# Weights cast by GpSimd's DMAs instead of by GpSimd: attention and MLP on one core

## The chip, the cores and the metric

The kernel runs on one core of a Trainium2 chip. The metric is the device time of one execution in microseconds. Before the change the median of three runs is 236.49 us (236.44 to 236.9).

## The reference

The program is an attention with a sliding window and four sink positions, followed by a two-layer MLP. All inputs and the output are fp32.

```python
scores = (q @ k.T) / sqrt(64)                  # q, k, v: 4 batches, 8 heads, 768 positions, 64
keep = (key < 4) | ((0 <= query - key) & (query - key < 128))
a = softmax(where(keep, scores, -1e9))
x = heads side by side of (a @ v)              # 3072 tokens x 512
h = x @ w_in                                   # w_in 512 x 2048
g = h * sigmoid(1.702 * h)
out = g @ w_out                                # w_out 2048 x 512
```

## The kernel before

**Blocks.** The 3072 tokens are worked in 12 blocks of 256, three to a batch. For a block, q, k and v are loaded as fp32 (`load`, three DMAs of 512 KB on SP's queue; block 0 in smaller pieces over SP and ACT), rounded to fp16 by casts (`qk16`, `v16`), and then per pair of heads: q and k are transposed on TensorE (L446) and copied from PSUM into `qkT` (L263), the sinks' scores (L474) and the window's scores (L513) are multiplied, ScalarE takes exponentials (L482, L530), VectorE multiplies with a 0/1 mask (L539, L543), TensorE multiplies with V (L573), VectorE divides by the row sums (L587, L589), and the result is transposed (L596) and copied into `xT` (L263). The sinks' keys and values of a batch are kept by small GpSimd copies (`ks` L466, `vs` L422).

**MLP.** `mm1` (L630) forms h for 256 tokens, eight groups of 256 features, 8 matmuls each; ScalarE takes tanh (L642), VectorE forms g from it (`stt`, L644). `mm2` (L780) multiplies g with `w_out16` for blocks 0, 1 and 11. Blocks 2 to 10 use seven products instead of eight (`mm2_seven`, L705): it needs four sums of blocks of g per block of tokens (L675, into `sm`) and, once, four sums of quarters of w_out. `sums` makes these in 16 instructions (L658, into `wt1` to `wt4`), four quarters long, each when the two weight loads that it reads are in.

**Weights.** w_in and w_out are 4 MB each. `weights` loads them in eight DMAs of 1 MB on SP's queue as fp32 into four staging places, `w32`, which are the later space of two `gT` and two `sm` buffers, and two GpSimd casts for each round them into `w_in16` and `w_out16`. `LOADS` gives the order: blocks 0 and 1, weights 0 to 3 (w_in), weights 4, 6, 5, 7 (w_out), block 2, and so on.

**The plan.** Nothing here runs in the order of the source. Each operation is an `Op` with its dependencies, the engines that may run it with an assumed duration and latency, and a priority worked out from its block (`nominal`, 16,600 ns a block). `Plan.run` simulates the engines, always places the operation that can start first, among those within 20 ns the one of the best priority, chooses an engine where there are several (`plan.any`), and gives out PSUM banks. The resulting order is written out as a fixed order for each engine; what an operation waits for on the chip follows from its data. The plan models DMA with a common clock (`dma_free`) and a list `landed` that keeps at most eight in flight. The loads are chained in order of priority (`behind`). Before block 0's work arrives TensorE runs dummy matmuls (L840). Three lists say which engines may cast: `CAST_QK`, `CAST_V` (from block 2 on GpSimd alone) and `COPY`, the copies from PSUM into `qkT` and `xT` (VectorE or ScalarE).

Of the kernel before, what the change touches and what calls it, by code (L numbers as in the profile page):

```python
# [9 lines left out]
FP32 = mybir.dt.float32  # L10
# [25 lines left out]
LANES = 8  # L36

COLD = 4700.0
ENGINES = ("PE", "ACT", "DVE", "POOL", "SP")


class Plan:
# [14 lines left out]
    def run(self, warm=None, warm_until=0.0, late_bank=0.0):  # L57
        for o in self.ops:
            o.left = len(o.deps)
            for d in o.deps:  # L60
                d.users.append(o)
        free = {e: 0.0 for e in ENGINES}
        ready = {e: [o for o in self.ops if e in o.engs and not o.left] for e in ENGINES}

        bank_free = {b: 0.0 for b in range(self.n_banks)}
        if late_bank:
            bank_free[self.n_banks - 1] = late_bank

        count = {c: {i: 0.0 for i in range(n)} for c, n in self.limits.items()}
        dma_free = 0.0  # L70
        landed = []
        order = []
        todo = len(self.ops)

        def after(d, e):
            if d.eng != e or isinstance(d.engs[e][1], tuple):
                return d.end + HOP.get((d.eng, e), 50)
            return d.start + d.engs[e][0] + (0 if d.eng == "PE" else 60)

        def could(o, e):  # L80

            if o.behind and o.behind.start is None:
                return None, None
            s = max([free[e]] + [after(d, e) for d in o.deps])
            if isinstance(o.engs[e][1], tuple) and len(landed) >= LANES:
                s = max(s, landed[-LANES])
            if not o.acq:
                return s, s
            cls, n = o.acq
            times = sorted(bank_free.values())  # L90
            places = sorted(count[cls].values())
            if len(times) < n or len(places) < n:
                return s, None
            return s, max(s, times[n - 1], places[n - 1])

        while todo:
            best = None
            for e in ENGINES:
                found = sorted(
                    [(*could(o, e), o) for o in ready[e]], key=lambda x: (x[2].prio, x[2].seq)  # L100
                )
                keep, held_from = [], None
                for s0, s, o in found:
                    if s0 is None:
                        continue
                    if o.acq and o.acq[1] > 2 and (s is None or s > s0):

                        held_from = s0 if held_from is None else min(held_from, s0)
                        if s is not None:
                            keep.append((s, o))  # L110
                        continue
                    if s is None or (o.acq and held_from is not None and s >= held_from):
                        continue
                    keep.append((s, o))
                if not keep:
                    continue
                first = min(s for s, _ in keep)
                s, o = min(((s, o) for s, o in keep if s <= first + 20), key=lambda x: (x[1].prio, x[1].seq))
                lat = o.engs[e][1]
                key = s if len(o.engs) == 1 else s + lat - min(x[1] for x in o.engs.values())  # L120
                if best is None or key < best[0]:
                    best = (key, s, o, e)
            if best is None:
                raise RuntimeError("no operation can be planned")
            _, s, o, e = best
            dur, lat = o.engs[e]
            if e == "PE" and warm and s < warm_until:
                t = max(free["PE"], 300.0)
                while t + 110 < s:
                    order.append((t, -1, warm, e))  # L130
                    t += 107 if t < COLD else 57
            for x in o.engs:
                ready[x].remove(o)
            o.eng, o.start = e, s
            if o.acq:
                cls, n = o.acq
                o.banks, o.places = [], []
                for _ in range(n):
                    b = min((b for b in bank_free if bank_free[b] <= s), key=lambda b: (bank_free[b], b))
                    del bank_free[b]  # L140
                    o.banks.append(b)
                    p = min((p for p in count[cls] if count[cls][p] <= s), key=lambda p: (count[cls][p], p))
                    del count[cls][p]
                    o.places.append(p)
            free[e] = s + dur
            if isinstance(lat, tuple):
                dma_free = max(s + 2000, dma_free) + lat[0]
                o.end = dma_free + (500 if lat[0] < 500 else 1100)
                landed.append(o.end)
            else:  # L150
                o.end = s + lat
            for owner, i in o.rel:
                t = o.end + 80
                bank_free[owner.banks[i]] = t
                count[owner.acq[0]][owner.places[i]] = t
            for u in o.users:
                u.left -= 1
                if not u.left:
                    for x in u.engs:
                        ready[x].append(u)  # L160
            order.append((s, o.seq, o.fn, e))
            todo -= 1
        order.sort(key=lambda x: (x[0], x[1]))
        return [(fn, e) for _, _, fn, e in order]
# [7 lines left out]
def kernel(  # L172
# [22 lines left out]
    NS = NF // 2  # L195
    scale = float(1.0 / np.sqrt(Dh))
    PAIRED_FROM, RR = 2, 3
    RS, RQ, RV, RKT, RA, RXN, RX, RG, RSM, RTH, RO, RW = 3, 2, 4, 3, 6, 3, 3, 4, 2, 3, 4, 4

    SEVEN_FROM = 2  # L200
    NH = NF // 2
# [5 lines left out]
    def ring(name, n, shape, dt):  # L207
# [27 lines left out]
    sm = ring("sm", RSM, (P, 4, NH, P), FP16)  # L235
    osb = ring("osb", RO, (P, d_model), FP32)
    bank = [psp.tile([P, 512], FP32, name=f"bank{i}") for i in range(8)]


    stage = [("gT", RG - 1 - n, gT[RG - 1 - n].rearrange("p f t -> p (f t)")) for n in range(RW - RSM)] + [  # L240
        ("sm", n, sm[n].rearrange("p s f t -> p (s f t)")) for n in range(RSM)]
    w32 = [t.bitcast(FP32).rearrange("p (c f) -> p c f", c=4) for _, _, t in stage]

    plan = Plan(8, {"s": 4, "k": 1, "t": 2, "a": 2, "x": 2, "h": RTH, "o": 3})
    op = plan.op
# [61 lines left out]
    o_table = op("ACT", 1300, 1400, lambda: nc.scalar.activation(out=dummy, in_=zero[:, 0:8], func=AF.Exp),  # L307
                 [o_zero], prio=NEVER + 8, kind="const")

    CAST_W = ["POOL"] * 8  # L310
    CAST_QK = ["DVE ACT POOL", "DVE POOL"] + ["POOL"] * (NK - 2)
    CAST_V = ["POOL ACT DVE", "POOL ACT"] + ["POOL"] * (NK - 2)
    COPY = ["DVE ACT"] * NK

    o_win, o_wout = {}, {}
    loads = []

    def weights(n_th, j, at):
        dst = w32[n_th % RW]
        war = reuse(*stage[n_th % RW][:2])  # L320
        if j < 4:
            src = moe_w_in[:, bass.ts(j, 512)].rearrange("(c p) f -> p c f", p=P)
        else:
            src = moe_w_out[bass.ts(j - 4, 512), :].rearrange("(c p) f -> p c f", p=P)
        o_l = op("SP", 450, (3000,), lambda: nc.sync.dma_start(dst, src), war, prio=at, kind="w")
        loads.append(o_l)
        for n in range(2):
            if j < 4:
                c = slice(512 * j + 256 * n, 512 * j + 256 * n + 256)
                to, fr = w_in16[:, :, c], dst[:, :, bass.ts(n, 256)]  # L330
            else:
                to, fr = w_out16[:, 4 * (j - 4) + 2 * n : 4 * (j - 4) + 2 * n + 2], dst[:, 2 * n : 2 * n + 2]
            o = plan.any(cast(1024, CAST_W[j]), lambda e, to=to, fr=fr: copy(e, to, fr), [o_l], prio=at, kind="cw")
            uses(*stage[n_th % RW][:2], o)
            (o_win if j < 4 else o_wout)[2 * (j % 4) + n] = o


    L = 16600.0
    LOADS = ["a0", "a1", "w0", "w1", "w2", "w3", "w4", "w6", "w5", "w7", "a2"]

    SLABS = (0, 1, 4, 5, 2, 3, 6, 7)

    def load_at(x):
        return NEVER + 10 * LOADS.index(x) + 3 if x in LOADS else 10000.0 + (int(x[1:]) - 3) * L
# [6 lines left out]
    def load(k):  # L351
# [17 lines left out]
        else:  # L369
            for e, src in enumerate((q, k_ap)):  # L370
                def f(e=e, src=src):
                    nc.sync.dma_start(
                        dst[:, e], src[b, :, t0 : t0 + TB].rearrange("h (p i) d -> p h i d", i=2)
                    )
                o = op("SP", 450, (1800,), f, war, prio=prio + 0.1 * e, kind="load")
                loads.append(o)
                for p in range(NP):
                    lq[p, e] = o
# [35 lines left out]
                o_cv[k].append(o)  # L414
                uses("s32", sl, o)
        if r == 0:
            w0 = [o_win[0], o_win[1]]

            def f():
                for t in range(2):  # L420
# [238 lines left out]
                deps = [o_wout[c], o_wout[NS // 2 + c]] + [o_wt[d, c] for d in {"2": "3", "4": "2"}.get(n, "")]  # L659
                o_wt[n, c] = plan.any(SUM_W, f, deps, prio=nominal(SEVEN_FROM, 0), kind="wt")  # L660

    SUM_W = {"POOL": (1000, 1100), "DVE": (340, 430)}
    o_sm = {}

    def mm2_seven(k):
# [143 lines left out]
                    o_d = op(eng, 500, (800.0 / len(moves) / parts,), f, [o_c], prio=prio, kind="out")  # L809
                    uses("osb", oi, o_d)  # L810

    for n_, x_ in enumerate([x for x in LOADS if x[0] == "w"]):
        weights(n_, int(x_[1:]), load_at(x_))
    for k_ in range(NK):
        load(k_)
        for p_ in range(NP):
            front(k_, p_)
        for ps_ in [(0,), (1,), (2,), (3,)] if k_ < PAIRED_FROM else [(0, 1), (2, 3)]:
# [62 lines left out]
```

## Time and profile before

| | before |
|---|---|
| median of three runs | 236.49 us |
| the profiled execution's own time | 236.4 us |
| its span, first to last instruction | 234.7 us |
| TensorE busy (PE) | 222.2 us, 95% |
| VectorE busy (DVE) | 190.3 us, 81% |
| ScalarE busy (ACT) | 140.9 us, 60% |
| GpSimd busy (POOL) | 98.6 us, 42% |
| mean granted TensorE clock | 0.992 |
| DMA | 33.98 MB, 145 GB/s on average |

Times in the lines of the profile are microseconds from the start of the span, unless marked as ns. PE is TensorE's matmuls, PEld its weight loads, which run beside them. A line of a timeline or of the chain has its start, its duration, the engine and the kernel's line; "x16" counts instructions. Back to back, a matmul's start follows the last one's by less than the duration that is shown for one. L263 is the helper `copy`, so all casts and copies carry that line and are told apart by their tiles.

### The profile page before, as it was taken

The page shows a single profiled execution, that of the slowest core. Times are in us where ns is not written, and L with a number is a line of the kernel's source. Part 1 is how long each engine was busy: PE and PEld are TensorE (multiplying, and loading weights), DVE is VectorE, ACT ScalarE, POOL GpSimd, SP SyncE. Part 2 cuts the span into 40 slices and gives each one's busy share as a digit, 9 for nine tenths or more (in the row PEclk, how much of TensorE's full clock was granted, in tenths as well). Part 3 has the DMA queues.
Part 4 walks back from the last instruction along what each step waited for, and adds up shares of the span by engine and source line. Part 5 has one row for each costly group of instructions (what it writes and reads, how often), then busy time and mean ns, then how long its engine had stood idle before and what let it go on. Part 6 is the DMA issues. An engine that isn't in the chain of part 4 may idle for free.

```text
span 234.7 us, 6390 instructions
## 1 busy us (share of the span) xinstructions
PE 222.2 (95%) x2534; PEld 183.0 (78%) x2534; DVE 190.3 (81%) x412; ACT 140.9 (60%) x293; POOL 98.6 (42%) x163
## 2 busy tenths in 40 slices
PE   8876999959999999999999999999999999999994
PEld 7654886526788888888789889888888888888863
DVE  6788979976899988988979879889969869878520
ACT  3749562536688838838648838838567757635320
POOL 5658889971899960358521441243300000000000
PEclk9999999979999999999999999999999999999999
DMA  6999999999879994644284004004003003003042
GB/s 169 292 357 387 382 383 287 288 302 274 223 191 295 250 232 90 176 100 89 74 197 92 0 3 89 4 1 94 0 13 82 0 14 78 3 17 78 0 92 89
DMA packets 45743, 33.98 MB, mean 145 GB/s; under 512 B 1552, under 2 KB 38672, under 8 KB 45712
## 3 DMA queue, kind: packets, MB, share of 16 engines
q1 hardware_dynamic: 44480, 32.90, 52.0%
q10 hardware_dynamic: 1232, 0.66, 1.0%
q8 instruction: 20, 0.33, 0.6%
q14 instruction: 11, 0.09, 0.1%
HBM read 27.26 MB, written 6.29 MB: 143 GB/s over the span
## 4 chain that ended last, share of the span: by engine, by line
PE 75%; DVE 17%; ACT 3%; DMA 2%; issue 1%; ACTq 0%
PE bank L630 29%; PE bank L705 22%; PE bank L780 6%; PE bank L573 5%; DVE wt L658 5%; PE bank L513 4%; PE bank L446 4%; DVE gT L644 3%; DVE sm L675 2%; PE bank L596 2%; DMA qk<-in_k_dram 2%; DVE at L539 2%; ACT at L530 2%; DVE at L543 1%; PE bank L474 1%
## 5 line engine op out<-in xcount | busy, mean ns | idle before, releaser
L630 PE MATMUL bank<-xT,w_in 128*128 128x256 f16 x768 | 101.7, 273 | 0.0
L642 ACT ACTIVATE th<-bank 128x512 f16<-128x512 f32 x96 | 57.6, 601 | 49.6 <-PE bank L630 46.0
L630 PEld LDWEIGHTS <-w_in 128*128 128x128 f16 x768 | 72.1, 98 | 10.3 <-issue 1.3
L644 DVE SCALAR_TENSOR_TENSOR gT<-th,bank 128x512 f16<-128x512 f16 x96 | 64.9, 679 | 9.0 <-ACT th L642 8.7
L530 ACT ACTIVATE at<-bank 128x512 f16<-128x512 f32 (+1 forms) x96 | 49.1, 569 | 11.8 <-PE bank L513 11.2
L263 POOL CAST qk<-qk 128x512 f16<-128x512 f32 (+1 forms) x42 | 28.9, 722 | 27.9 <-PE bank L446 25.7
L263 POOL CAST v<-v 64x512 f16<-64x512 f32 x43 | 30.3, 705 | 8.8 <-PE bank L573 6.4
L705 PE MATMUL bank<-wt,sm 128*128 128x256 f16 x216 | 30.6, 273 | 0.4 <-DVE sm L675 0.3
L705 PEld LDWEIGHTS <-sm 128*128 128x128 f16 x288 | 26.5, 98 | 4.8 <-DVE sm L675 0.9
L539 DVE TENSOR_TENSOR at<-at,mask 128x1024 f16<-128x1024 f16 x32 | 23.5, 753 | 6.6 <-ACT at L530 6.6
L780 PE MATMUL bank<-w_out,gT 128*128 128x512 f16 (+1 forms) x112 | 24.5, 358 | 0.0
L573 PE MATMUL bank<-v,at 128*128 128x65 f16 x352 | 21.5, 193 | 2.0 <-DVE at L539 1.8
L705 PEld LDWEIGHTS <-gT 128*128 128x128 f16 x216 | 20.1, 98 | 2.3 <-issue 0.3
L573 PEld LDWEIGHTS <-at 128*128 128x128 f16 x352 | 17.3, 97 | 4.0 <-DVE at L539 2.2
L589 DVE TENSOR_TENSOR xn<-bank,rcp 128x256 f16<-128x256 f32 x48 | 19.8, 417 | 0.4
L466 POOL COPY ks<-qkT 64x4 f16<-64x4 f16 x32 | 9.5, 297 | 24.8 <-ACT qkT L263 19.7
L705 PE MATMUL bank<-w_out,gT 128*128 128x256 f16 x144 | 19.7, 273 | 0.0
L446 PE MATMUL bank<-ident,qk 128*128 128x128 f16 x192 | 18.9, 225 | 0.5 <-DVE qk L263 0.4
L730 DVE SCALAR_TENSOR_TENSOR osb<-bank,osb 128x256 f32<-128x256 f32 x45 | 18.4, 409 | 0.6 <-PE bank L705 0.6
L482 ACT ACTIVATE ats<-bank 128x256 f16<-128x256 f32 x32 | 12.4, 388 | 9.2 <-PE bank L474 7.8
L446 PEld LDWEIGHTS <-qk 128*128 128x128 f16 x192 | 14.0, 100 | 3.1 <-DVE qk L263 1.1
L780 PEld LDWEIGHTS <-gT 128*128 128x128 f16 x112 | 10.9, 101 | 6.9 <-issue 1.3
(53 smaller groups left out, 274.4 us busy)
## 6 DMA issues: line engine op xcount, KB each, us to landing
v<-in_v_dram SPq DMA_DIRECT2D x12, 512.0 KB, 7.2
out_dram<-osb SPq DMA_DIRECT2D x45, 128.0 KB, 2.4
qk<-in_q_dram SPq DMA_DIRECT2D x11, 512.0 KB, 5.2
qk<-in_k_dram SPq DMA_DIRECT2D x11, 512.0 KB, 6.7
gT<-in_moe_w_in_dram SPq DMA_DIRECT2D x2, 1024.0 KB, 10.1
sm<-in_moe_w_in_dram SPq DMA_DIRECT2D x2, 1024.0 KB, 13.0
gT<-in_moe_w_out_dram SPq DMA_DIRECT2D x2, 1024.0 KB, 8.0
sm<-in_moe_w_out_dram SPq DMA_DIRECT2D x2, 1024.0 KB, 8.5
```

Source lines behind the costliest of these rows:

```text
L263: {"POOL": nc.gpsimd.tensor_copy, "DVE": nc.vector.tensor_copy, "ACT": nc.scalar.copy}[e](out=out, in_=in_)
L446: nc.tensor.transpose(ps[:, e, :, i, :], c16[:, i, e, 2 * p : 2 * p + 2].rearrange("s h d -> s (h d)"), ident)
L530: nc.scalar.activation(out=A[:, i, 0:W], in_=f32(o_s, 2 * n + i)[:, 0:W], func=AF.Exp, scale=scale)
L539: nc.vector.tensor_tensor(out=a_, in0=a_, in1=m_[:, 2 * P :].unsqueeze(1).to_broadcast((P, 4, 2 * P)), op=ALU.mult,)
L573: nc.tensor.matmul(avp()[:, j, i], a_, v_, start=(n == 0), stop=(n == len(mms) - 1))
L589: o_n = op("DVE", 333, 425, lambda: nc.vector.tensor_tensor(out=X[:, p].rearrange("s j (h d) -> s j h d", h=2), in0=avp()[:, :, :, 0:D], i ...
L630: nc.tensor.matmul(f32(holder[0])[:, bass.ts(e, TB)], w_in16[:, c, bass.ts(Fi, P)], X[:, c], start=(c == 0), stop=(c == NP - 1),)
L642: o_t = op("ACT", 477, 600, lambda first=first: nc.scalar.activation(out=th[first.places[0]], in_=f32(first), func=AF.Tanh, scale=0.851), ...
L644: o_g[k, s] = op("DVE", 595, 690, lambda first=first, s=s: nc.vector.scalar_tensor_tensor(out=g[:, 2 * s : 2 * s + 2].rearrange("p a t -> ...
L705: nc.tensor.matmul(f32(holder[bank_of])[:, 0:HM], x[:, Fi], w[:, Fi], start=first and Fi == 0, stop=Fi == NH - 1, skip_group_check=True)
L730: f, ns = (lambda: nc.vector.scalar_tensor_tensor(out=out, in0=src(), scalar=0.5, in1=add, op0=ALU.mult, op1=ALU.add)), (333, 425)
L780: nc.tensor.matmul(f32(holder[0])[:, 0:w], g[:, Fi, bass.ts(j, P)], w_out16[:, Fi, c], start=(n + h == 0), stop=(n + h == NS),)
```

## The change

- `weights` issues each weight's DMA from GpSimd's queue (`nc.gpsimd.dma_start`), with the fp32 weight in HBM as its source and the fp16 tile as its destination. The staging places, their ring and the 16 casts go. The eight DMAs wait for block 0's four v casts (`o_cv[0]`).
- The first load of block 2 (q) waits for a GpSimd copy of one element, which reads what weight 5's DMA writes and writes into the load's destination (`FIRST_LATE`).
- The plan treats any GpSimd operation and VectorE's operations of the kinds in `SHARED` as excluding each other in time (`held`), and doesn't count GpSimd's DMAs in `landed`.
- The 16 sums of weights may run on VectorE only; one of them ran on GpSimd before.
- The copies of blocks 1 to 3 from PSUM (`COPY`) may run on VectorE only.

The order of the instructions of all engines is planned anew. In it VectorE takes three of block 0's four v casts (two before) and all four q/k casts of block 1 (three before), ScalarE all four v casts of block 1 (two before). Some products with w_in of block 0 stand earlier on TensorE, between the scores of block 1, and the products of attention with V of block 1 later.

```diff
+SHARED = ("mask", "sum", "wt", "cqk", "cv")
...
+        held = {"DVE": 0.0, "POOL": 0.0}
...
+        def locks(o, e):
+            return e == "POOL" or e == "DVE" and o.kind in SHARED
+
...
-            if isinstance(o.engs[e][1], tuple) and len(landed) >= LANES:
+            if isinstance(o.engs[e][1], tuple) and e != "POOL" and len(landed) >= LANES:
                 s = max(s, landed[-LANES])
+            if locks(o, e):
+                s = max(s, held["DVE" if e == "POOL" else "POOL"])
...
+            if locks(o, e):
+                held[e] = s + dur - (130 if e == "POOL" else 0)
...
-                landed.append(o.end)
+                if e != "POOL":
+                    landed.append(o.end)
...
-    CAST_W = ["POOL"] * 8
...
-    COPY = ["DVE ACT"] * NK
+    COPY = ["DVE ACT"] + ["DVE"] * 3 + ["DVE ACT"] * (NK - 4)
...
-    def weights(n_th, j, at):
-        dst = w32[n_th % RW]
-        war = reuse(*stage[n_th % RW][:2])
+    def weights(j, at):
+
         if j < 4:
-            src = moe_w_in[:, bass.ts(j, 512)].rearrange("(c p) f -> p c f", p=P)
+            dst, src = w_in16[:, :, bass.ts(j, 512)], moe_w_in[:, bass.ts(j, 512)]
         else:
-            src = moe_w_out[bass.ts(j - 4, 512), :].rearrange("(c p) f -> p c f", p=P)
-        o_l = op("SP", 450, (3000,), lambda: nc.sync.dma_start(dst, src), war, prio=at, kind="w")
+            dst, src = w_out16[:, bass.ts(j - 4, 4)], moe_w_out[bass.ts(j - 4, 512), :]
+        o_l = op("POOL", 1200, (3000,), lambda: nc.gpsimd.dma_start(dst, src.rearrange("(c p) f -> p c f", p=P)),
+                 o_cv[0], prio=at, kind="w")
         loads.append(o_l)
         for n in range(2):
-            if j < 4:
-                c = slice(512 * j + 256 * n, 512 * j + 256 * n + 256)
-                to, fr = w_in16[:, :, c], dst[:, :, bass.ts(n, 256)]
-            else:
-                to, fr = w_out16[:, 4 * (j - 4) + 2 * n : 4 * (j - 4) + 2 * n + 2], dst[:, 2 * n : 2 * n + 2]
-            o = plan.any(cast(1024, CAST_W[j]), lambda e, to=to, fr=fr: copy(e, to, fr), [o_l], prio=at, kind="cw")
-            uses(*stage[n_th % RW][:2], o)
-            (o_win if j < 4 else o_wout)[2 * (j % 4) + n] = o
-
+            (o_win if j < 4 else o_wout)[2 * (j % 4) + n] = o_l
...
+    FIRST_LATE = 2
...
+                if k == FIRST_LATE and e == 0:
+
+                    war = war + [op("POOL", 80, 180, lambda: nc.gpsimd.tensor_copy(
+                        out=dst[0:1, 0, 0, 0, 0:1], in_=w_out16[0:1, 4, 0:1]), [o_wout[2]], prio=prio, kind="gate")]
...
-    SUM_W = {"POOL": (1000, 1100), "DVE": (340, 430)}
+    SUM_W = {"DVE": (340, 430)}
...
-    for n_, x_ in enumerate([x for x in LOADS if x[0] == "w"]):
-        weights(n_, int(x_[1:]), load_at(x_))
     for k_ in range(NK):
         load(k_)
+        if k_ == 0:
+            for j_ in range(8):
+                weights(j_, load_at(f"w{j_}"))
```

More of the change, by code (lines that the diff above doesn't have):

```diff
@@ L197 @@
     PAIRED_FROM, RR = 2, 3
-    RS, RQ, RV, RKT, RA, RXN, RX, RG, RSM, RTH, RO, RW = 3, 2, 4, 3, 6, 3, 3, 4, 2, 3, 4, 4
+    RS, RQ, RV, RKT, RA, RXN, RX, RG, RSM, RTH, RO = 3, 2, 4, 3, 6, 3, 3, 4, 2, 3, 4
     SEVEN_FROM = 2
@@ L237 @@
     bank = [psp.tile([P, 512], FP32, name=f"bank{i}") for i in range(8)]
-    stage = [("gT", RG - 1 - n, gT[RG - 1 - n].rearrange("p f t -> p (f t)")) for n in range(RW - RSM)] + [
-        ("sm", n, sm[n].rearrange("p s f t -> p (s f t)")) for n in range(RSM)]
-    w32 = [t.bitcast(FP32).rearrange("p (c f) -> p c f", c=4) for _, _, t in stage]
     plan = Plan(8, {"s": 4, "k": 1, "t": 2, "a": 2, "x": 2, "h": RTH, "o": 3})
@@ L416, in load @@
         if r == 0:
-            w0 = [o_win[0], o_win[1]]
             def f():
```

## The prediction

> **What bounds the kernel now.** I read the page first: TensorE is busy 95% of the span and carries 75% of the chain, VectorE 17%. So time can only be won where TensorE stops or runs slowly. The table of busy time by stretch finds that place. Its columns are the stretch, its length, then busy microseconds and instructions of PE, PEld, DVE, ACT and POOL, the granted clock, the DMA share and GB/s.
>
> ```profile
> 30.00:35.00 5.00, 5.00 (x44) 4.10 (x43) 3.98 (x7) 2.81 (x6) 4.33 (x5) 1.00 1.05 386
> 100.00:120.00 20.00, 19.82 (x226) 16.91 (x224) 17.84 (x40) 11.38 (x26) 12.06 (x24) 1.00 0.47 114
> 46.00:48.00 2.00, 0.57 (x8) 0.26 (x7) 2.00 (x4) 1.41 (x3) 2.00 (x4) 1.00 1.21 291
> 48.00:50.00 2.00, 0.13 (x4) 0.13 (x5) 1.82 (x4) 0.00 (x0) 1.90 (x3) 0.97 1.18 285
> 50.00:52.00 2.00, 2.00 (x17) 1.36 (x15) 0.66 (x2) 0.73 (x2) 1.23 (x2) 0.50 1.19 309
> 52.00:54.00 2.00, 2.00 (x9) 0.79 (x8) 1.39 (x3) 0.66 (x3) 0.00 (x0) 0.68 0.83 258
> ```
>
> From 25 us on TensorE is full, with one hole at 46 to 50 us; behind it the granted clock is 0.50 and 0.68 for 4 us. From 80 to 220 us it is idle 0.4 us in all. The waits between 9 and 56 us name the hole, and the chain of that stretch (start, length, what) says what filled VectorE:
>
> ```profile
> PE bank L513 <- DVE qkT L263: 3.3, 1, 3.3
> 37.09 5.08 DVE wt L658 x6
> 44.09 3.33 DVE wt L658 x5
> 48.02 1.46 DVE wt L658 x2
> 49.48 0.35 DVE qkT L263
> 49.87 0.61 PE bank L513 x6
> ```
>
> The scores of block 2 (L513) waited 3.3 us for a copy (qkT) that stood on VectorE behind the sums of weights (wt). Those sums are slow. By shape:
>
> ```profile
> L658 DVE TENSOR_TENSOR wt<-w_out 128x512 f16<-128x512 f16 x7 | 5.0, 749 | 0.0
> L658 DVE TENSOR_TENSOR wt<-wt,w_out 128x512 f16<-128x512 f16 x4 | 3.6, 932 | 0.0
> L658 DVE TENSOR_TENSOR wt<-w_out,wt 128x512 f16<-128x512 f16 x4 | 3.1, 815 | 0.0
> ```
>
> The timelines of VectorE and GpSimd show why. The mask product, which also has two SBUF inputs, took 1.45 us apiece beside GpSimd's casts and 0.68 us beside none, so the sum's half size should cost about 0.35 to 0.4 us alone:
>
> ```profile
> 18.68 2.91 DVE L539 TENSOR_TENSOR at<-at,mask 128x1024 f16<-128x1024 f16 x2 [0.65 <-ACT at L530]
> 56.51 0.68 DVE L539 TENSOR_TENSOR at<-at,mask 128x1024 f16<-128x1024 f16 x1
> 18.57 2.48 POOL L263 CAST w_in<-gT 128x1024 f16<-128x1024 f32 x2 [2.43 <-DMA gT<-in_moe_w_in_dram]
> 29.25 2.03 POOL L263 CAST w_out<-gT 128x1024 f16<-128x1024 f32 x2 [0.65 <-DMA gT<-in_moe_w_out_dram]
> 37.43 2.22 POOL L263 CAST w_out<-sm 128x1024 f16<-128x1024 f32 x2 [0.16 <-DMA sm<-in_moe_w_out_dram]
> 39.59 3.05 POOL L263 CAST qk<-qk 128x512 f16<-128x512 f32 x4
> ```
>
> The bracket is idle time and what ended it: GpSimd waits for DMA, so these starts are landings. First weight 18.57, eighth 37.43: 18.86/7 = 2.69 us per MiB, 387 GB/s, as in the 386 GB/s row above. Until 37 us the weights' DMA sets the pace as much as TensorE.
>
> **The change, part by part.**
>
> *Casts removed.* Sixteen casts leave GpSimd, 5.2+4.5+4.4+4.1 = 18.2 us by their rows, and two us between landing and use. Only the first two (to 21.05) gate TensorE, whose first MLP product starts at 21.09.
>
> *Weights on GpSimd's queue.* Eight DMAs stand on POOL behind block 0's small copies and wait for its four v casts. VectorE does three of these now: from 10.09, 3 x 0.5 = about 11.7 us. [...] Before, the same bytes stood behind block 1's loads on SP, which landed at 14.57, with DMA saturated; so the first weight again lands near 18.3 if the pace holds. The pace of a DMA that casts is in no row. Nearest: 2.69 us per MiB for the same 2 KB reads, and 3.6 us for 512-byte traffic (291 GB/s at 46 us), since writes become 1 KB. Below, halved writes could give 1.35; above, half rate gives 5.4. I take 2.7, because reads, their sizes and their count stay.
> [...]
>
> *Head.* In the built order TensorE now does 8 products of block 0 ahead of the third pair's scores, 8 ahead of the fourth's and 32 before any attention-times-V of block 1. Those 32 need weight 2 (lands about 23.8). From there, at 0.109 us per product (16 in 1.75) and 0.216 per output product (2 in 0.43): 16 products to 25.6, 24 AV to 26.6, 12 products (weight 3, 26.5) to 27.9, transposes and 24 AV to 29.1, 4 to 29.5, 8 output products (weight 4, 29.2) to 31.3, then 64 products 7.0, 24 output products 5.2, four of block 1 0.9: 44.4, where block 2's transposes stand. Before they began at 44.66. Block 1's own attention starts later: four q/k casts, now all on VectorE behind the xT copies, end near 16.9 instead of 15.0, and ACT takes four v casts (0.62 each); that lag is covered by the 32 products. I cost the head at 0, ends -0.7 and +3.
>
> *The held load.* Block 2's q load waits on SP for a one-element POOL copy that waits for weight 5 (seventh in order, about 34.5). Behind that copy on POOL stand only block 2's own casts; behind the load on SP, all later loads. Weight 7 ends 2.7 us later, q and k (1 MB at 290 GB/s) 3.6 after that, receipt 1: k at 41.8, cast (0.73) at 42.5. Needed at 44.4, so hidden by 1.9 us; each 0.1 us of pace costs about 1 us once this cover is gone.
>
> *Sums.* All 16 on VectorE instead of 15 (the one on POOL was 1.15 us). GpSimd only waits from about 24 to 39 us, so the first eight cost about 0.4 (bounds 0.35 and 0.9). The second eight start with weight 7 at 37.3 beside GpSimd's late casts: 4 x 0.4 + 4 x 0.8 = 4.8, and three gate products (0.6 apiece back to back) 1.8, so VectorE is free at 43.9, in time for the copy at 44.8. At 0.85 apiece it is 45.9: a stall of 1.1.
>
> *The plan taking turns.* It orders, it adds no wait on the chip. From 80 us TensorE is full either way; ends -0.4 and +1, I take 0. COPY on VectorE alone for blocks 1 to 3 moves copies (0.42 and 0.30) from ACT, which had time, to VectorE; covered by the 3.5 us that the sums give back.
>
> **Sum.** The hole: -3.3, of which I leave 0.2. The slow clock behind it: 2 x 0.50 + 2 x 0.32 = 1.6, of which I leave 0.4. Together -4.3. The profiled execution is 236.4 us (span 234.7, 1.7 around it); 232.1, and 0.1 more for the median of 236.49: 232.2.
>
> **Rivals.**
> (a) *The casting DMAs are slow.* At pace p the first weight lands near 15.6+p, weight 5 six later, k at p+4.6 behind that, cast 0.7: 20.9+8p against 44.4. The gain of 4.3 is gone at p = 3.5 us (300 GB/s), and 3.6 gives 237. Half rate, 5.4, puts block 2's transposes near 64 us, 19.7 late, less the 4.3: about 252. For: writes of 1 KB and a conversion that no row prices. Against: reads unchanged, 387 GB/s.
> (b) *GpSimd and VectorE block each other at the issue.* The eight DMAs hold GpSimd from 11.7 us; behind them is the vs copy (2.04), needed by AV at 25.6. At over (25.6-2.0-11.7)/8 = 1.5 us per issue TensorE waits. SP's issues of the same transfers took 0.37 to 1.67; the plan writes 1.2. And if each of the four q/k casts at 15 us waits out one issue, block 1's scores come 4 x 1.2 = 4.8 us later, ahead of everything in TensorE's order: the gain of 4.3 is gone and the time is 236.5 + 0.5 = 237.
> [...]
> (c) *The hole moves.* The second half of the sums stays at 0.85 beside block 2's casts: 1.1 of stall and the low clock again 1.6; 234.5.
>
> **Chances.** Forecast with its own range 230.5 to 234: 0.48. (c) and paces of 3.1 to 3.4, 234 to 236: 0.14. (b), or a pace near 3.6, 236 to 240: 0.16. Slow DMAs, 240 to 255: 0.18. Better than 230.5, if the head gains: 0.04. About 0.2% is what a measurement tells from no change. Faster 0.61, same 0.04, slower 0.35. The range is 230.5 to 246: under it 0.04, over it some 0.12.
>
> **What would show it.** Right: no wait of L513 for qkT near 46 us, wt sums near 0.4 to 0.6 us, clock 1.00 at 44 to 54 us, weight landings 2.7 us apart, DMA near 385 GB/s from 15 to 35 us. Wrong: output products or block 2's transposes waiting for a weight or qk load (a); AV of block 1 waiting for vs, or q/k casts well above 0.6 us at 13 to 20 us (b); wt still over 0.8 us (c).

## The result

| | before | after |
|---|---|---|
| median | 236.44 us (235.53 to 237.63) | 233.98 us (232.32 to 235.79) |
| ratio, 95% interval | | 0.991 [0.988, 0.993] |
| profiled execution, its span | 236.4, 234.7 us | 233.38, 231.7 us |
| granted clock, mean | 0.992 | 0.991 |

The kernel became faster by 0.9%, where 232.2 us (1.8%) was forecast. On the chips of the later runs the kernel before spread from 232.4 to 238.5 us, at mean granted clocks from 1.000 down to 0.976, and the ratios leave its disturbed executions out, so kernels that ran together are best compared by their medians with each other.

**The hole is gone.** The table of busy time by stretch of the changed kernel; its columns are the stretch, its length, busy us and instructions of PE, PEld, DVE, ACT and POOL, the granted clock, the DMA share and GB/s:

```profile
18.00:20.00 2.00, 2.00 (x24) 1.28 (x24) 0.69 (x2) 1.71 (x5) 0.32 (x1) 0.78 1.24 206
20.00:22.00 2.00, 2.00 (x13) 1.22 (x13) 1.66 (x3) 1.23 (x3) 0.00 (x0) 0.50 1.25 207
22.00:24.00 2.00, 2.00 (x23) 1.20 (x20) 0.69 (x1) 1.60 (x4) 0.00 (x0) 0.87 1.24 206
...
48.00:50.00 2.00, 2.00 (x26) 1.25 (x21) 1.21 (x3) 2.00 (x6) 1.88 (x5) 1.00 1.18 286
50.00:52.00 2.00, 2.00 (x37) 1.41 (x36) 1.68 (x4) 1.86 (x5) 1.82 (x2) 1.00 1.18 295
```

From 46 to 50 us TensorE is full (busy 5.00 of the 5 us from 45 to 50) where it was busy 0.70 us before, and the clock behind it is 1.00 where it was 0.50. But there is a new stretch of low clock at 19 to 23 us, 2 x (0.22 + 0.50 + 0.13) = 1.7 us, where the kernel before had 1.00 throughout.

The sums of weights, by shape (columns: count, busy us, mean ns, idle time ahead):

```profile
L660 DVE TENSOR_TENSOR wt<-w_out 128x512 f16<-128x512 f16 x8 | 3.5, 472 | 0.0
L660 DVE TENSOR_TENSOR wt<-w_out,wt 128x512 f16<-128x512 f16 x4 | 2.4, 589 | 0.0
L660 DVE TENSOR_TENSOR wt<-wt,w_out 128x512 f16<-128x512 f16 x4 | 2.3, 620 | 0.0
```

Sixteen take 8.2 us instead of 11.7 for fifteen, and the wait of the scores for qkT near 46 us has left the list of waits. The chain of work shows what came in the head:

```profile
15.67 1.94 DVE qk L269 x4
17.61 0.34 DVE qkT L269
...
19.99 1.71 PE bank L632 x8
...
46.46 0.45 PE bank L448 x8
```

Block 1's q and k casts stand on the chain until 17.6 us, and the eight products behind them take 1.71 us, twice the 0.87 us that eight take elsewhere, at a clock of 0.50 (20 to 22 us).

The weights' DMAs, by their line, and GpSimd's timeline behind them (the bracket is idle time and what ended it):

```profile
L329 POOL DMA_DIRECT2D w_in<-in_moe_w_in_dram x4: 747/765/878, 10.1 to 12.5; - x4
L329 POOL DMA_DIRECT2D w_out<-in_moe_w_out_dram x4: 780/792/903, 13.2 to 15.4; - x4
DMA to landing us min/median/max: 7.4/14.3/20.6
```

```profile
33.48 0.35 POOL L376 CAST qk<-w_out 1x1 f32<-1x1 f16 x1 [15.16 <-DMA w_out<-in_moe_w_out_dram]
38.25 1.36 POOL L269 CAST qk<-qk 128x512 f16<-128x512 f32 x2 [4.42 <-DMA qk<-in_q_dram]
41.14 1.18 POOL L269 CAST qk<-qk 128x512 f16<-128x512 f32 x2 [1.53 <-DMA qk<-in_k_dram]
```

The first weight lands at 10.1 + 7.4 = 17.5 us and the eighth at 15.4 + 20.6 = 36.0: 2.64 us per MiB read. Block 2's k is cast by 42.3 us; its transposes start at 46.46.

**Where the time went.** I counted how much TensorE had lost by a given moment: the elapsed time less the products started by then at full clock, 0.109 us for 256 columns (from 16 products in 1.75 us); dummy matmuls are no products. The figure is an estimate, and only its differences between kernels at the same moment are used. By 46 us the changed kernel had lost 16.3 us and the kernel before 15.1; by 60 us 16.3 and 19.7; by 80 us 16.5 and 20.0. So the head lost 1.2 us and the stretch of the hole won 4.6 us.

TensorE's last product ends at 227.5 us where it ended at 231.4, 3.9 us earlier, and yet the spans differ by only 3.0. The last products of the chain, before and after (start, length, what):

```profile
224.44 6.96 PE bank L780 x48
220.60 6.96 PE bank L782 x48
```

From the end of the last product to the end of the span it is 3.29 us before and 4.13 us after. All ten profiles of kernels with the casting DMAs have 4.11 to 4.13 us there, and all four without them 3.29 us. So the change makes the kernel's end 0.8 us longer. In the traces some 0.3 us of it is a longer row of waits on SyncE and the rest falls on GpSimd's closing steps; which part of the change causes it was not tested.

### The profile page after: what moved, and what is told of

It reads as the page before. It is cut to its first block, busy times and chain, and to the rows that moved or that the text cites. A ratio compares the mean times of both kernels' runs of the same rounds, so it can differ in the third digit from the quotient of the medians.

```text
span 231.7 us, 6375 instructions
## 1 busy us (share of the span) xinstructions
PE 221.7 (96%) x2536; PEld 183.6 (79%) x2536; DVE 188.7 (81%) x424; ACT 138.9 (60%) x286; POOL 81.3 (35%) x151
## 4 chain that ended last, share of the span: by engine, by line
PE 79%; DVE 15%; DMA 2%; issue 1%; ACT 1%; ACTq 0%; DVEq 0%
PE bank L632 31%; PE bank L707 22%; PE bank L782 9%; PE bank L575 5%; PE bank L515 4%; PE bank L448 4%; DVE gT L646 3%; PE bank L598 2%; DVE xn L591 2%; DVE sm L677 2%; DMA qk<-in_k_dram 2%; DVE at L541 2%; DVE at L545 2%; PE bank L476 1%; DVE qk L269 1%
## 5 line engine op out<-in xcount | busy, mean ns | idle before, releaser
L632 PE MATMUL bank<-xT,w_in 128*128 128x256 f16 x768 | 103.3, 274 | 0.0
L269 POOL CAST qk<-qk 128x512 f16<-128x512 f32 (+1 forms) x41 | 27.2, 696 | 33.0 <-PE bank L448 25.0
L269 POOL CAST v<-v 64x512 f16<-64x512 f32 x40 | 28.0, 701 | 9.9 <-PE bank L575 7.7
L707 PE MATMUL bank<-wt,sm 128*128 128x256 f16 x216 | 29.9, 273 | 0.6 <-DVE xT L269 0.6
L541 DVE TENSOR_TENSOR at<-at,mask 128x1024 f16<-128x1024 f16 x32 | 22.6, 714 | 6.0 <-ACT at L532 6.0
L782 PE MATMUL bank<-w_out,gT 128*128 128x512 f16 (+1 forms) x112 | 23.6, 349 | 0.0
L707 PEld LDWEIGHTS <-gT 128*128 128x128 f16 x216 | 20.5, 98 | 2.1
L575 PEld LDWEIGHTS <-at 128*128 128x128 f16 x352 | 17.5, 98 | 2.0 <-issue 0.9
L732 DVE SCALAR_TENSOR_TENSOR osb<-bank,osb 128x256 f32<-128x256 f32 x45 | 18.5, 410 | 0.6 <-PE bank L707 0.6
L707 PE MATMUL bank<-w_out,gT 128*128 128x256 f16 x144 | 18.8, 273 | 0.0
L448 PEld LDWEIGHTS <-qk 128*128 128x128 f16 x192 | 13.8, 99 | 3.9 <-DVE qk L269 2.2
L468 POOL COPY ks<-qkT 64x4 f16<-64x4 f16 x32 | 8.6, 269 | 22.0 <-DVE qkT L269 15.6
L269 DVE COPY qkT<-bank 128x512 f16<-128x512 f16 x33 | 13.5, 416 | 3.4 <-PE bank L448 3.3
```

What stands on the lines that cost most here:

```text
L269: {"POOL": nc.gpsimd.tensor_copy, "DVE": nc.vector.tensor_copy, "ACT": nc.scalar.copy}[e](out=out, in_=in_)
L448: nc.tensor.transpose(ps[:, e, :, i, :], c16[:, i, e, 2 * p : 2 * p + 2].rearrange("s h d -> s (h d)"), ident)
L541: nc.vector.tensor_tensor(out=a_, in0=a_, in1=m_[:, 2 * P :].unsqueeze(1).to_broadcast((P, 4, 2 * P)), op=ALU.mult,)
L575: nc.tensor.matmul(avp()[:, j, i], a_, v_, start=(n == 0), stop=(n == len(mms) - 1))
L632: nc.tensor.matmul(f32(holder[0])[:, bass.ts(e, TB)], w_in16[:, c, bass.ts(Fi, P)], X[:, c], start=(c == 0), stop=(c == NP - 1),)
L707: nc.tensor.matmul(f32(holder[bank_of])[:, 0:HM], x[:, Fi], w[:, Fi], start=first and Fi == 0, stop=Fi == NH - 1, skip_group_check=True)
```

## The experiments

The theory after the result: the hole gave all that was forecast, and what the head lost was lost to the granted clock, which fell because TensorE had little to do from 14 to 18 us (busy 1.61 of the 4). The rivals: the plan's turns as such cost the head, or the gain comes from another part than the casting DMAs.

### Keeping TensorE busy in the head

```diff
-    order = plan.run(warm=warm, warm_until=12000.0, late_bank=12500.0)
+    order = plan.run(warm=warm, warm_until=18500.0, late_bank=18500.0)
```

> The changed kernel with dummy matmuls filling TensorE's planned gaps until 18.5 us instead of 12, and the last PSUM bank given out from 18.5 us. Theory A: the 1.7 us that the changed kernel loses in its head is the low granted clock at 18 to 24 us (0.78, 0.50, 0.87), which follows TensorE's idling at 14 to 18 us. Then the clock stays at 1.00, the 32 products of block 0 start 1.2 to 1.7 us earlier than 23.9, and the time falls to about 232.4 (0.984 of before). Theory B: the loss is that block 1's q/k casts end late and the order has the scores behind them; the clock only shows it. Then the 32 products start within 0.5 us of 23.9 and the time stays near 234.0 (0.990).

232.04 us (231.47 to 232.88), ratio 0.988 [0.984, 0.993]; the mean granted clock 0.995 to 1.000. Its busy time by stretch:

```profile
18.00:20.00 2.00, 2.00 (x28) 1.51 (x24) 1.13 (x3) 2.00 (x6) 0.00 (x0) 1.00 1.28 216
20.00:22.00 2.00, 2.00 (x25) 1.28 (x24) 1.60 (x3) 2.00 (x5) 0.00 (x0) 1.00 1.21 199
```

The stretch in which the changed kernel ran at 0.50 runs at 1.00, the median is 1.9 us below the changed kernel's, and block 2's transposes start at 44.55 instead of 46.46 us. Matmuls that compute nothing gave back what the head had lost. Not all of it need be the clock's: in this profile block 1's q and k casts also ended 0.5 us earlier, at 17.1 instead of 17.6 us.

### The plan's turns

Without turns between VectorE's work and the issues of GpSimd's DMAs (turns with its other work stay):

```diff
-            return e == "POOL" or e == "DVE" and o.kind in SHARED
+            return e == "POOL" and o.kind != "w" or e == "DVE" and o.kind in SHARED
```

> The changed kernel, but its plan no longer excludes GpSimd's eight DMA issues from VectorE's casts, masks and sums (other GpSimd work it still does). In the order the four q/k casts of block 1 move ahead, between block 0's divisions. Theory: the plan's turns pushed these casts behind the issues for nothing. Then they stay at 0.4 to 0.6 us each, end near 15 instead of 17.6, the scores start near 16.5 instead of 18.2, weights land as before the edit, and the time falls to about 232.2 (0.982 of before). Rival (b) of the prediction, issues and casts block each other: the casts take 0.8 us or more or the issues stretch well over 0.8 us each, weight 5 lands later than 33.3, and the time is 234 or more (0.990 up).

234.29 us (233.73 to 235.44), ratio 0.998 [0.995, 1.001], clock 1.00. Block 1's four casts of q and k now stand among the issues, from 12.78 us on, and take 0.39 to 0.74 us each; none waited out an issue of 0.77 us or more. But the transfers did worse. A line of the list of waits, and busy time by stretch with DMA's GB/s at the end (the changed kernel had 200 and 205 in these two):

```profile
PEld L632 <- DMA w_in<-in_moe_w_in_dram: 1.0, 1, 1.0
```

```profile
14.00:15.00 1.00, 0.92 (x19) 0.69 (x15) 0.97 (x4) 0.63 (x2) 1.00 (x3) 1.00 1.13 159
...
16.00:17.00 1.00, 0.62 (x7) 0.31 (x9) 0.95 (x3) 0.33 (x2) 0.90 (x3) 1.00 1.12 154
```

The first weight landed at 19.1 us instead of 17.5, and TensorE waited for it. In the new order ScalarE's four v casts, which stand ahead of block 1's exponentials, also run 1.6 us later (16.9 to 19.5 us), and TensorE was idle 1.3 of the 6 us from 18 to 24. So the kernel kept its clock and still gained nothing. Without the turns the transfers were slower, but this run does not part that loss from the one through ScalarE. The first weight came 1.6 us later here; for what reason was not tested.

### The plan without the casting DMAs

The kernel before with the turns, all sums on VectorE and the copies of blocks 1 to 3 on VectorE; weights staged and cast as before:

```diff
+        held = {"DVE": 0.0, "POOL": 0.0}
...
+        def locks(o, e):
+            return e == "POOL" or e == "DVE" and o.kind in SHARED
...
-    COPY = ["DVE ACT"] * NK
+    COPY = ["DVE ACT"] + ["DVE"] * 3 + ["DVE ACT"] * (NK - 4)
...
-    SUM_W = {"POOL": (1000, 1100), "DVE": (340, 430)}
+    SUM_W = {"DVE": (340, 430)}
```

> The kernel before with the rest of the change and without its DMAs: staging, SP loads and GpSimd's 16 casts stay, but the plan takes turns, all 16 sums are on VectorE and the copies of blocks 1 to 3 too. Theory: the hole at 46 to 50 us comes from GpSimd's weight casts beside the sums and behind them block 2's casts; with the casts still there the sums stay at 0.7 us or more, the hole stays at 2 us or more and the time is 235.5 to 240 (0.996 to 1.015). Rival: the order gave the gain; then the hole is under 1 us and the time is 234.5 or less (below 0.993).

236.3 us (235.71 to 237.41), ratio 1.007 [1.004, 1.010], beside a median of 236.84 us for the kernel before in the same runs: no gain by medians. Its eight sums of two quarters of w_out still took 646 ns each on average, 0.1 us less than before. Against the expectation TensorE was full from 46 to 50 us; but a hole came elsewhere, at 22 to 26 us, where TensorE was busy 1.96 of 4. Its second half, by stretch:

```profile
24.00:26.00 2.00, 0.76 (x7) 0.43 (x5) 2.00 (x5) 0.60 (x1) 1.95 (x3) 1.00 1.05 384
```

VectorE and GpSimd are both full in it. With GpSimd still casting the weights, this plan moved the hole and did not remove it. So the plan, the sums and the copies without the casting DMAs do not give the gain.

### The casts taken from GpSimd, without new DMAs

```diff
-    CAST_W = ["POOL"] * 8
+    CAST_W = ["ACT"] * 8
```

> The kernel before with the 16 casts of weights on ScalarE instead of GpSimd, nothing else. Theory: sums are slow only where GpSimd casts beside them; GpSimd is now free until block 2's load, so the sums that run before its casts fall to 0.35 to 0.45 us, and their mean from 0.81 to under 0.6; the hole shrinks to 1.5 us or less. ScalarE pays 16 x 0.9 = 14 us at 18 to 38 us, where it also has exponentials and tanh, so the time may be anywhere from 234 to 240. Rival: the sums are slow or late for another reason; then their mean stays above 0.7 us.

236.69 us (236.16 to 238.28), ratio 1.008 [1.004, 1.012]. Its sums by shape, and its busy time by stretch:

```profile
L658 DVE TENSOR_TENSOR wt<-w_out 128x512 f16<-128x512 f16 x7 | 2.7, 420 | 0.1
```

```profile
18.00:20.00 2.00, 1.95 (x22) 1.02 (x21) 1.02 (x2) 2.00 (x5) 0.00 (x0) 0.59 1.05 388
...
45.00:50.00 5.00, 5.00 (x51) 3.35 (x50) 4.42 (x10) 2.88 (x7) 4.83 (x7) 1.00 1.06 277
```

With GpSimd quiet a sum costs 0.42 us where it cost 0.75, and the hole at 46 to 50 us is gone without any change to the DMAs. The first step of the mechanism, that GpSimd's casts slow the sums, is shown by this. The second, that the slow sums made the hole, is shown less cleanly: by the count above TensorE had lost 5.8 us more than in the kernel before by 46 us, which gave VectorE that much more time. The gain is lost again because ScalarE is now full in the head: TensorE was idle 3.9 of the 13 us from 22 to 35, and the clock fell in the head too (0.56 and 0.59 from 16 to 20 us). A cast took 1.05 to 1.08 us on ScalarE, where 0.9 was expected.

### The copies, the held load, and a better plan

The changed kernel ran again beside three variants on one chip.

> The changed kernel again, unedited, on the chip of the runs of this call, as their measure: 233.5 to 234.5 us, 0.985 to 0.993 of before. If the low clock in its head is what spreads its times (232.3 at a mean clock of 1.000, 235.1 to 235.6 at 0.982 in the first comparison), the same holds here.

234.52 us (233.19 to 235.65), ratio 0.990 [0.987, 0.994]. Its profile had the clock at 0.50 from 17.2 to 24 us, twice as long as the first one.

Copies free again:

```diff
-    COPY = ["DVE ACT"] + ["DVE"] * 3 + ["DVE ACT"] * (NK - 4)
+    COPY = ["DVE ACT"] * NK
```

> The changed kernel with the copies of blocks 1 to 3 free again to go to ScalarE, as before the change. Theory: VectorE had room for them after the sums became fast, so this part is worth little: within 0.7 us of the changed kernel either way. Rival: it matters, because VectorE is full in the stretch up to 60 us; then the chain of that stretch shows copies, and the time differs by 1 us or more.

235.02 us (234.34 to 236.09), ratio 0.993 [0.990, 0.995]; 0.5 us above the changed kernel in the medians. The intervals overlap, so no effect of this part is shown, and one of up to about 1 us is not excluded.

Block 2's load not held back:

```diff
-    FIRST_LATE = 2
+    FIRST_LATE = -1
```

> The changed kernel without the one-element copy that holds block 2's loads until weight 5 has landed. Theory: block 2's loads then share the DMA engines with the weights from about 11 us on; weights land later by the 1.5 to 4.5 MB that get ahead of them, up to 4 to 10 us for the last, TensorE waits for weights 1 to 3 at 22 to 30 us and the time is 1.5 to 6 us longer than the changed kernel (235.5 to 240). Rival: the queues are served in turn so that the weights hardly suffer; then the time is within 0.7 us of the changed kernel.

237.77 us (236.48 to 238.16), ratio 1.010 [1.006, 1.014]: 3.25 us above the changed kernel.

```profile
26.00:28.00 2.00, 0.76 (x8) 0.69 (x8) 1.86 (x3) 1.08 (x3) 0.71 (x2) 1.00 1.19 214
...
30.00:35.00 5.00, 3.15 (x46) 2.69 (x47) 3.70 (x13) 1.19 (x2) 2.30 (x4) 1.00 1.20 216
```

Block 2's loads, issued from 9.0 us on instead of 33.9, now run beside the weights, and TensorE waits for 3.2 of the 9 us from 26 to 35. The held load is not only covered, as I had it; without it the kernel would be slower than before.

The plan with the issue and the transfer as long as measured, block 1's v casts on GpSimd, and the prolonged dummy matmuls:

```diff
-    CAST_V = ["POOL ACT DVE", "POOL ACT"] + ["POOL"] * (NK - 2)
+    CAST_V = ["POOL ACT DVE", "POOL"] + ["POOL"] * (NK - 2)
...
-        o_l = op("POOL", 1200, (3000,), lambda: nc.gpsimd.dma_start(...
+        o_l = op("POOL", 780, (2650,), lambda: nc.gpsimd.dma_start(...
...
-    order = plan.run(warm=warm, warm_until=12000.0, late_bank=12500.0)
+    order = plan.run(warm=warm, warm_until=18500.0, late_bank=18500.0)
```

> The kernel with dummy matmuls until 18.5 us, and besides: the plan takes 780 ns for an issue on GpSimd (0.75 to 0.9 us in the traces) and 2650 ns for a weight's transfer, and block 1's four v casts go to GpSimd behind its issues instead of to ScalarE. Theory: block 1's exponentials no longer wait behind 2.5 us of v casts on ScalarE, the 32 products start earlier than in the kernel with dummy matmuls alone, and the time falls from 232.0 to about 231. Rival: GpSimd's v casts at 18 to 21 us slow the mask products beside them to 1.2 us or more, or TensorE then waits for weights 1 and 2; then it stays at 232 or is longer.

230.72 us (230.59 to 231.29), ratio 0.975 [0.972, 0.977], clock 0.996 to 1.000. It beats both kernels.

### Which of its edits helped

The same without the dummy matmuls:

```diff
-    CAST_V = ["POOL ACT DVE", "POOL ACT"] + ["POOL"] * (NK - 2)
+    CAST_V = ["POOL ACT DVE", "POOL"] + ["POOL"] * (NK - 2)
...
-        o_l = op("POOL", 1200, (3000,), lambda: nc.gpsimd.dma_start(...
+        o_l = op("POOL", 780, (2650,), lambda: nc.gpsimd.dma_start(...
```

> The changed kernel with two numbers of its plan set to what the traces show (780 ns for the issue of a weight, 2650 ns for its transfer) and block 1's v casts put on GpSimd, but without the additional dummy matmuls. It separates the two edits of the run that gave 230.7 us. Theory, the granted clock: TensorE is still idle for most of 14 to 18 us, because the q and k casts still come behind GpSimd's issues, so the clock still falls to 0.5 to 0.8 between 16 and 24 us, and the time stays at 232.5 to 234. Rival, the exponentials: what helped was that ScalarE starts block 1's exponentials earlier because it no longer casts v; then the time comes to about 231 without any dummy matmul, whatever the clock.

230.99 us (230.18 to 232.93), ratio 0.980 [0.974, 0.986]. I expected 232.5 or more; the time is the rival's. But the premise of my expectation had failed: with shorter issues in the plan one q/k cast ran at 13.35 us and the others ended at 16.7, five more dummy matmuls stood ahead of them, TensorE was busy 2.66 of the 4 us from 14 to 18 (1.61 in the changed kernel), and the clock stayed at 1.00. So this run didn't tell the two apart, and each edit was run alone.

```diff
-        o_l = op("POOL", 1200, (3000,), lambda: nc.gpsimd.dma_start(...
+        o_l = op("POOL", 780, (2650,), lambda: nc.gpsimd.dma_start(...
```

> The changed kernel with only the two numbers of its plan set to what the traces show (780 ns for the issue of a weight, 2650 ns for its transfer). The run that held both edits (230.99 us) kept its granted clock at 1.00, with TensorE busy 2.66 of the 4 us from 14 to 18 us where the changed kernel had 1.61. Theory, the granted clock: the shorter issues let the plan put the q and k casts earlier and five more dummy matmuls before them, so this edit alone keeps the clock at 1.00 and gives about 2 us, 231.5 to 232.5, as the prolonged dummy matmuls did. Rival, the exponentials: this edit alone leaves ScalarE's four v casts in front of them, so it gives under 0.7 us, 233.3 or more, and the other edit alone gives the gain.

231.83 us (231.6 to 232.23), ratio 0.981 [0.978, 0.984]. Its clock over the stretch in question:

```profile
16.00:18.00 2.00, 0.77 (x9) 0.45 (x8) 2.00 (x5) 1.93 (x4) 1.84 (x4) 1.00 1.23 201
18.00:20.00 2.00, 2.00 (x28) 1.48 (x28) 0.96 (x3) 1.95 (x5) 0.56 (x2) 1.00 1.24 206
```

```diff
-    CAST_V = ["POOL ACT DVE", "POOL ACT"] + ["POOL"] * (NK - 2)
+    CAST_V = ["POOL ACT DVE", "POOL"] + ["POOL"] * (NK - 2)
```

> The changed kernel with only block 1's v casts moved from ScalarE to GpSimd. Theory, the granted clock: the q and k casts stay where they were, TensorE is still busy for less than 2 of the 4 us from 14 to 18 us, the clock falls to 0.5 to 0.8 behind it, and the time stays at 232.7 to 234, about 1 us gained at most from the earlier exponentials. Rival, the exponentials: this edit alone gives about 231, whatever the clock.

233.34 us (232.2 to 234.03), ratio 0.986 [0.982, 0.990].

```profile
16.00:18.00 2.00, 0.89 (x10) 0.47 (x12) 1.95 (x5) 0.00 (x0) 1.79 (x4) 0.72 1.24 206
18.00:20.00 2.00, 2.00 (x20) 1.14 (x20) 0.43 (x1) 1.47 (x3) 1.82 (x4) 0.50 1.24 206
```

TensorE was busy 2.23 of the 4 us with the first edit alone and kept its clock; with the second alone it was busy 1.69 and lost it. The first gives about 2 us, as the dummy matmuls did; the second, ScalarE's four v casts gone from ahead of the exponentials, 0.6 to 0.8 (233.98 to 233.34, and 231.83 to 230.99). These pairs ran on different chips, on which the medians of the kernel before differ by 0.2 and 0.6 us, so the size of this second part is not settled.

### The control

The prolonged dummy matmuls in the kernel before:

```diff
-    order = plan.run(warm=warm, warm_until=12000.0, late_bank=12500.0)
+    order = plan.run(warm=warm, warm_until=18500.0, late_bank=18500.0)
```

> The kernel before, with the dummy matmuls prolonged to 18.5 us of the plan as in the run that kept the clock up. A control. Theory, the granted clock: the kernel before already has a granted clock of 1.00 from 14 to 20 us, so there is nothing to win, and it stays within 0.7 us of its median of about 236.5. Rival: the dummy matmuls help whatever the clock was, for example by moving block 1's products, and the kernel before gains the 2 us as well, 234.5 or less.

235.84 us (233.74 to 237.9), ratio 0.997 [0.993, 1.001], beside a median of 236.0 us for the kernel before: no gain, as the theory has it. Its profiled execution is one of its best, 233.74 us at a mean clock of 0.999. It still has the hole, which there lasts from 46.0 to about 48.7 us; this time the clock didn't fall behind it:

```profile
48.00:49.00 1.00, 0.26 (x6) 0.17 (x5) 0.68 (x2) 0.00 (x0) 0.94 (x3) 1.00 1.21 290
...
50.00:51.00 1.00, 1.00 (x7) 0.46 (x5) 1.00 (x2) 0.97 (x2) 0.78 (x2) 1.00 1.22 292
```

In these two profiles the same hole costs its length alone or its length and the slow clock as well; the last section sets them side by side. Four of this kernel's twelve executions kept a clock of 0.998 or more and took 233.7 to 234.5 us, three of the 74 of the kernel before that ran beside the later experiments; so the dummy matmuls may help it now and then, but not in the median.

**All of it in one table.** TensorE's time lost by 26, 46, 60 and 80 us (the count of the result's section), the end of its last product, and the span:

| kernel | 26 | 46 | 60 | 80 | last product | span |
|---|---|---|---|---|---|---|
| before | 15.2 | 15.1 | 19.7 | 20.0 | 231.4 | 234.7 |
| after | 15.7 | 16.3 | 16.3 | 16.5 | 227.5 | 231.7 |
| after, dummy matmuls to 18.5 us | 13.8 | 14.4 | 14.4 | 14.7 | 225.6 | 229.8 |
| after, issue and transfer as measured | 14.2 | 14.8 | 14.8 | 15.5 | 226.4 | 230.5 |
| after, v casts on GpSimd | 16.5 | 17.2 | 16.8 | 17.1 | 228.1 | 232.2 |
| after, the last two together | 13.4 | 13.7 | 13.6 | 13.6 | 224.6 | 228.7 |
| after, load not held | 16.2 | 21.3 | 21.0 | 21.1 | 232.1 | 236.2 |
| before, dummy matmuls | 14.6 | 14.7 | 17.3 | 17.6 | 228.7 | 232.0 |

At 80 us each row's distance from the first is that of the last products to within 0.5 us: but for the 0.8 us at the end, what tells these kernels apart happens before. The two runs that only kept the clock up lie 1.9 and 1.5 us below the changed kernel at 46 us; the held load is worth 5.0 us there.

## Why the prediction was right, and where it was not

- *The hole, -3.3 and the slow clock behind it, -1.6, of which 0.6 was left.* Right. By the table of stretches the kernel before was idle 3.3 us from 46 to 60 us and lost 1.7 at a lower clock, 5.0 together; the changed kernel is idle 0.07 us there, so nothing of the 0.6 stayed. The count gives 4.6 us for the same stretch.
- *The pace of the casting DMAs, 2.7 us per MiB.* Measured 2.64. Rival (a) is out. One premise was wrong: the chip did not hold these DMAs until block 0's v casts were done. The first issue starts at 10.14 us and the casts end at 12.02; only the plan puts one behind the other. The first weight landed at 17.5 us where I had 18.3. The eight in a row went at 397 GB/s of bytes read. No run shows the 3.1 us per MiB at which one of the chances begins.
- *The head at 0, ends -0.7 and +3.* This is the step that failed, though the 1.2 us that it cost lie inside these ends. I walked through it in products at full clock and asked only whether the weights and VectorE came in time. They did, at 17.5 and 33.5 us. But I had block 1's q and k casts end near 16.9 us (it was 17.6), 1.9 later than before, and called that lag covered by the 32 products. The products that cover it only stand behind block 1's first scores; ahead of them, from 14 to 18 us, TensorE had 1.6 us of work, and the clock fell to 0.50 for 3.4 us. That is 1.7 us by the stretches, 1.2 us net by the count at 46 us. Block 2's transposes came at 46.46 us instead of 44.4. I had 16 of the 32 products done by 23.8 us; in the trace all 32 begin at 23.93, and 16 products are 1.75 of these 2.1 us. With the dummy matmuls the 32 begin at 21.84 and block 2's transposes at 44.55.
- *The held load hidden by 1.9 us.* Hidden by more: k was cast at 42.3 us, as forecast (42.5), and needed at 46.46. No run shows the 1 us that this sum has as receipt: k had landed by 41.14 us, where its cast starts, and in the kernel before the last output (issued at 231.88, 1.9 us to landing) landed at about 233.8, some 0.4 us after the last bytes moved (by 233.4). That the held load is needed itself (3.25 us of time without it) was no step of mine.
- *The sums, 0.4 us each in the first half, 0.4 and 0.8 in the second.* By VectorE's timeline three in a row took 1.09 us (0.36 each) with GpSimd idle, and two took 1.57 (0.78 each) beside its casts, as forecast. Rival (c)'s slow second half is there in part and made no stall.
- *Rival (b), the issue.* An issue took 0.77 us, not the 1.5 from which TensorE would wait, and no cast waited one out. Where the turns are dropped, it is the first weight that comes 1.6 us late. The plan's assumed 1.2 us per issue did harm in another way: with 0.78 in its place the plan puts casts and dummy matmuls earlier, and the clock holds.
- *The plan's turns and copies at 0.* By the count the changed kernel was 3.4 us ahead at 60 us, 3.5 at 80 and 3.9 at the last product, so nothing was lost behind the hole. The copies alone make 0.5 us in the medians, which is not settled.
- *The end of the kernel.* It stands in no term of mine. It became 0.8 us longer, 4.13 us behind the last product instead of 3.29.
- *Sum.* 1.2 for the head, -4.6 for the hole, -0.4 from 60 us to the last product and 0.8 for the end are -3.0, the difference of the spans, instead of -4.3. In the medians it is 2.5, and 233.98 lies at the upper edge of the 230.5 to 234 that the forecast gave itself. Executions differ in their mean clock: five of the changed kernel's fifteen have 0.982 or 0.983 where the profiled one has 0.991. Its only execution at 1.000 took 232.32 us, next to the 232.2 that was forecast with 0.4 us of slow clock left; that the two meet is partly luck, since the end's 0.8 us is not in the forecast.

Executions with a like mean clock can be set side by side, over all chips. At 0.988 to 0.995 the kernel before has a median of 235.56 us (32 executions beside the later runs) and the changed kernel 233.94 (12); at 0.981 to 0.987 it is 236.93 (26) and 235.22 (8). So 1.6 to 1.7 us of the gain is there at an equal loss of clock.

One thing stays open. In 3 of 74 executions beside the later runs the kernel before had a mean clock of 0.998 to 1.000 and took 232.4 to 232.8 us, no more than that one of the changed kernel. None of the three was profiled, so whether their hole was shorter isn't known, nor whether the change gains anything where the clock never falls.

## What to carry to other kernels

A gap in TensorE's work can cost more than its length: in this kernel a thin stretch of about 4 us (TensorE busy 1.6) was followed by 3.4 us at half clock, so count TensorE's work in every stretch of that length of the changed order, and not only who waits for whom. Compare also what follows the last product: here it took back 0.8 us that no stage of the work shows. A planner's assumed durations are part of the kernel: two numbers set to what the trace shows gave 2 us. When a change moves DMAs to another queue, look for the load that must be held back for it, since that can be worth more than the change (here 3.25 us against 2.5).

## What the runs showed that I had not expected

- **The low clock lasted 3.42 us, or twice that.** From 16 to 24 us in slices of 1 us, the share of clock lost is 0.44 + 0.50 + 0.50 + 0.27 = 1.71 us in the changed kernel, and in the run with v casts on GpSimd 0.06 + 6 x 0.50 + 0.36 = 3.42; behind the hole of the kernel before it is 0.06 + 3 x 0.50 + 0.15 = 1.71. At half clock that is 3.42, 6.84 and 3.42 us. The changed kernel's low clock lies at 19.13 to 22.54 us, that of the kernel before at 49.89 to 53.30. What sets this length was not tested.
- **A thin stretch did not always cost the same.** Behind the hole of the kernel before (TensorE busy 0.12 us from 46.47 to 49.88) the clock fell to 0.50 for 3.41 us. With the prolonged dummy matmuls TensorE was busy 0.26 us from 46 to 49, and the clock stayed at 1.00 in every slice up to 55 us. In the kernel before TensorE was also busy only 0.41 us from 18 to 20, and the clock stayed at 1.00 up to 49.8 us. The changed kernel's order lost 3.4 us of half clock in one profile and 6.8 in the other. What decides between these was not varied by itself.
- **TensorE need not be idle for it.** In the changed kernel the clock fell when it was busy 0.52, 0.28, 0.64 and 0.17 of the four 1 us slices from 14 to 18 us, and held with 0.54, 0.60 and 0.17 in the three from 15 to 18 behind a slice of 0.92 (the run with the issue as measured).
- **The GB/s of the casting DMAs are those of the bytes written.** The rows show 205 GB/s while the weights load, at 2.64 us per MiB of fp32 read: 397 GB/s read, half of it written. Writing half made them hardly faster: 2.64 us per MiB where the DMAs without a cast had 2.69.
